# First attention of a three-stage kernel: from a generator-driven order to a sorted list of timed events, one slot per head

## Chip, cores, metric

The kernel runs on one core of a Trainium2 chip, as a single launch. The metric is the device time of that launch in microseconds; lower is better. Five queues of one core matter here: PE (TensorE, matmuls, with its weight loads shown apart as PEld), DVE (VectorE), ACT (ScalarE), POOL (GpSimd), and SP (SyncE), which here only issues DMAs. Each takes its own instructions in order, and they meet at semaphores.

## The reference, cut to what matters

Four batches of 576 positions. Stage one is causal attention with 8 heads of 64 and a cumulated log decay. Stage two adds a rank-32 mix over positions and a wide feed-forward layer. Stage three is a second attention of four gated experts. Only stage one and the first part of stage two are touched.

```python
def _attn_ref(q, k, v, f):              # q, k, v: (4, 8, 576, 64); f: (4, 8, 576)
    scores = scale * np.matmul(q, k.transpose(0, 1, 3, 2))
    cum = np.cumsum(np.log(np.clip(f, 0.0001, 1.0)), axis=-1)
    decay = cum[:, :, :, None] - cum[:, :, None, :]
    scores = np.where(causal, -1000000000.0, scores + decay)
    attn = np.exp(scores - np.max(scores, axis=-1, keepdims=True))
    attn = attn / (np.sum(attn, axis=-1, keepdims=True) + 1e-09)
    return np.matmul(attn, v)

def _moe_ref(x, U, V, w_ch1, w_ch2):    # x: (4, 576, 512), w_ch1: (512, 2048)
    h = x.transpose(0, 2, 1) @ U @ V
    u = x + h.transpose(0, 2, 1)
    return u + np.maximum(u @ w_ch1, 0.0) @ w_ch2
```

The results have to be good to far more than 16 bits, so operands are split in a high and a low part and multiplied in three products.

## The kernel before, in words

**Units of work.** There are 32 heads, taken as 16 pairs: the two heads of a pair share one load of q and k (`qkt`), one of v (`vr`) and one tile `x` for their result. The work of a head is:

- *split*: ACT writes the high parts of q and k, SP issues three or four DMAs that move halves to the other partitions and bring the decay sums, POOL subtracts to get the low parts (`split_high`, `split_low`);
- *row maxima* (`row_max`): PE computes unshifted scores of the rows in two PSUM tiles, `ua` (2 matmuls) and `ub` (4 matmuls), DVE takes their maxima (L174, L189), PE turns these (`mt`), DVE makes the row `mr` (L196) and SP writes it by DMA into the last partition of `qa` (L198), so that the score matmul subtracts the maximum;
- *scores*: PE fills two PSUM tiles `sc`, the first with 5 matmuls, the second with 12 (L232); ACT takes the exponentials (L242, three of them) and their 16-bit high parts `ph` (L247); DVE subtracts to get the low parts (L248);
- *attend*: 45 small matmuls (L263 to L267) into `av`, then three DVE operations `den`, `rn`, `x` (the last is L316) that normalise.

`ua`, `ub` and both `sc` share one pair of PSUM buffers (tag `s2`) in turn, so each of the four waits for the reader of the one two before it.

**Per pair** come the scaling of v (`am`, `amt`, `ar`, `rsp`, `rs`, `vr`, `vh`, `vl`: seven short steps that go from DVE to PE and back twice) and the *mix* of stage two (`mix`): `gp` (5 products in 10 passes) from `x`, then `g`, then `up` (7 matmuls), `ustage`, and a store of 288 KB to `udram`, which ACT's queue issues.

**Beside it** run two things. The weights of the first two quarters of the feed-forward layer come as 16 blocks of 512 KB of 8-byte numbers, which ACT (2 passes) and DVE (L353, L354) turn into 4-byte ones; the first eight are then split by ACT and POOL. And from pair 5 on, *fills* are put between the steps on PE: one fill is 12 matmuls of 288 columns of the feed-forward layer, either a hidden tile (`hps`, L638, read by ACT and DVE) or an output tile (`cps`, L654, read by DVE). `GROUPS` says how many fills a pair has, 38 in all. After stage one the same stream of fills goes on without attention, the dense phase, in which the next quarter's operands are made ready, paced by the fills.

**What sets the order.** `first_batch` (pairs 0 to 3) and `later_batches` (pairs 4 to 15) are written as generators that are advanced step by step; PE keeps that order, the others (DVE, ACT, POOL, SP) are put in order by a scheduler that ranks what is ready. In the later pairs one copy of `qkt`, `vr` and `x` is in use, in the first four pairs two. In the later pairs the mix of a pair is put between the two score tiles of the head after next, and the blocks of weights come in bunches per pair: `WRATE` gives 2, 3 and 3 to pairs 2, 3, 4, one to each of pairs 5 to 12, and the rest are eight small maxima.

Of the kernel before, what the change touches and what calls it, by code (L numbers as in the profile page):

```python
# [8 lines left out]
F32 = mybir.dt.float32  # L9
# [9 lines left out]
P = 128  # L19
# [45 lines left out]
def kernel(  # L65
# [100 lines left out]
    def row_max(hb, mx, apart=False):  # L166

# [3 lines left out]
        for c0, c1 in ((0, HC), (HC, S)):  # L171
            nc.tensor.matmul(ua[:, c0 // HC, 0:HC], qa[0:AUG, M_LO[4]:S], ka[0:AUG, c0:c1],
                             start=True, stop=True)
        nc.vector.tensor_tensor_reduce(  # L174
            ua[:, :, 0:HC], ua[:, :, 0:HC],
            maskm[:].rearrange("p (c n) -> p c n", c=2), 1.0, NEG, OP.add, OP.max, mx[:, 4:5])
        if apart:
            yield
        ub = ps2.tile([P, 2, 512], F32, name="ub", tag="s2")
        where = {3: (0, 0), 0: (0, 448), 2: (1, 0), 1: (1, 320)}  # L180
        for t in (3, 2, 1, 0):
            bk, off = where[t]
            w = M_W[t]
            nc.tensor.matmul(ub[:, bk, off:off + w], hb.wide[0:AUG, t * P:t * P + P],  # L184
                             ka[0:AUG, 0:w], start=True, stop=True)
        for t in (3, 2, 1, 0):
# [5 lines left out]
        yield  # L192
        mt = psf.tile([NT, P], F32, name="mt", tag="f")
        nc.tensor.transpose(mt[:], mx[:], ident[:])
        mr = small.tile([NT, P], F32R, name="mr", bufs=2)
        cur["mr"] = nc.vector.tensor_scalar(mr[:], mt[:], PSCALE_LN / ISC, None, OP.subtract)  # L196
        row = f32(hb.wide[AUG:P, :]).rearrange("o (t p) -> o t p", p=P)
        cur["last"] = nc.sync.dma_start(row, f32(mr[:]))  # L198

# [8 lines left out]

    def scores(hb, exps, select=False):

        qa, qb, ka, kb = hb
        ph, pl = exps
        for u in range(2):
            ps = ps2.tile([P, 2, 512], F32, name="sc", tag="s2")
            if u == 0:
                pieces = ((0, 0, 0, HC, 0), (0, HC, 1, HC, 0))
            else:
                pieces = ((2, 256, 0, 320, 0), (3, 384, 0, 192, 320),
                          (1, 128, 1, 448, 0), (4, 512, 1, 64, 448))

            todo = []
            for some in (pieces[:-1], pieces[-1:]):
                todo += [(ka[:, jt * P:jt * P + P], qa[:, i0:i0 + w], bk, off, w)
                         for jt, i0, bk, w, off in some]
                todo += [(kb[:, jt * P:jt * P + P], qb[:, i0:i0 + w], bk, off, w)
                         for jt, i0, bk, w, off in some]
            if not select:
                todo += [(identb[:], maskt[:, 0:min(P, w)], bk, off, min(P, w))
                         for jt, i0, bk, w, off in reversed(pieces) if i0 == jt * P]
            banks = [t[2] for t in todo]  # L230
            for n, (wa, xa, bk, off, w) in enumerate(todo):
                nc.tensor.matmul(ps[:, bk, off:off + w], wa, xa, start=bk not in banks[:n],  # L232
                                 stop=bk not in banks[n + 1:])
            if u == 0:
                todo = ((ps[:, :, 0:HC], 0, S, ((0, P),)),)
            else:
                todo = ((ps[:, 0, :], S, 512, ((0, P), (320, P))),
                        (ps[:, 1, :], S + 512, 512, ((0, P), (448, 64))))
            for view, o0, n, diagonals in todo:
                pf = cur["pf"].tile([P, S], F32, name="pf")  # L240
                pfv = pf[:, 0:S].rearrange("p (c n) -> p c n", c=2) if u == 0 else pf[:, 0:n]
                nc.scalar.activation(pfv, view, AF.Exp, scale=ISC)  # L242
                for d0, w in diagonals if select else ():
# [27 lines left out]
    def value_scale(vr):  # L271
# [3 lines left out]
        yield  # L275
        at_ = psf.tile([1, P], F32, name="amt", tag="f")
        nc.tensor.transpose(at_[:], am[:], ident[:])
        counter[1] += 1
# [6 lines left out]
        yield  # L285

        rp = psf.tile([P, 1], F32, name="rsp", tag="f")
        nc.tensor.matmul(rp[:], every[:], full[:].bitcast(BF16)[:, 1:2], start=True, stop=True)
        rs = small.tile([P, 1], F32, name="rs")
# [3 lines left out]
    def value_parts(vr, rs, vh, vl):  # L293

        scaled = nc.vector.tensor_scalar(vr, vr, rs[:, 0:1], VEXP, OP.mult, OP.mult)
        nc.scalar.copy(vh[:, :, :, 0:64], vr)
        nc.gpsimd.tensor_tensor(vl[:], vr, vh[:, :, :, 0:64], OP.subtract)
        return scaled
# [33 lines left out]
    def narrow(wt, raw, n, p0=0, p1=P):  # L332


        lo, hi = raw[p0:p1, :, 0], raw[p0:p1, :, 1]
        wi = wt.bitcast(I32)
        nc.vector.tensor_scalar(wi, lo, 29, None, OP.logical_shift_right)
        nc.scalar.activation(f32(lo), f32(hi), AF.Copy, scale=2.0 ** -112)
        nc.vector.scalar_tensor_tensor(wi, lo, 3, wi, OP.logical_shift_left, OP.bitwise_or)
        nc.vector.scalar_tensor_tensor(wi, hi, -2147483648, wi, OP.bitwise_and, OP.bitwise_or)  # L340

    def low_bits(wt, raw):

# [12 lines left out]
    def load_quarter_steps(wp, q):  # L356
# [1274 lines left out]
```

## Time and profile before

| | |
|---|---|
| device time, median of 3 runs (lowest, highest) | 904.18 us (900.08, 904.35) |
| the profiled execution: its own time, its span | 904.51 us, 902.8 us |
| stage one: first exponential of head 0, of head 31, last matmul of the last mix | 21.72, 362.28, 377.1 us |
| mean distance from head to head in stage one | 340.56 us / 31 = 10.99 us |
| PE busy, DVE busy over the span | 780.2 us, 634.3 us |

The span is the time from the first to the last instruction; the execution's own time is 1.7 us longer. Busy time counts an engine as busy while at least one of its instructions runs. Matmuls overlap each other, so the cost of one is read from the distance of two starts, not from its duration. PEclk is the granted clock of TensorE, 1.00 being the full 2.4 GHz and 0.50 the lower level.

### The profile page before, as it was taken

What the parts mean: (1) busy time and instruction counts of PE and PEld (TensorE: products, weight loads), DVE (VectorE), ACT (ScalarE), POOL (GpSimd) and SP (SyncE); (2) the same over time, 40 slices, a digit from 0 to 9 for tenths busy, and PEclk for the clock granted to TensorE, in tenths of its full rate; (3) what the DMA queues carried; (4) which work ended last, traced back from release to release, by engine and by line L of the source; (5) the groups of instructions that cost most, each with busy time, mean ns of one, the idle gap of its engine ahead of it and who ended that gap; (6) DMA issues with size and microseconds to landing.
All of it is one profiled execution on the core that took longest, in us unless ns stands there. A gap on an engine that the chain in (4) does not pass through costs nothing.

```text
span 902.8 us, 19100 instructions
## 1 busy us (share of the span) xinstructions
PE 780.2 (86%) x7426; PEld 666.0 (74%) x7426; DVE 634.3 (70%) x1716; ACT 440.0 (49%) x852; POOL 211.5 (23%) x297
## 2 busy tenths in 40 slices
PE   3687576767877887989989999999999999889997
PEld 2676576666877786889767777777777888777764
DVE  6999986676567656279778737746653688887875
ACT  4587764455555554246262313311321267576674
POOL 9856753243433430000000100000001131011110
PEclk9997998999899999999999999999999999989999
DMA  6346653445444421159263231440010251412212
GB/s 189 111 111 175 177 160 103 112 131 170 112 137 132 125 72 40 31 190 311 78 194 100 93 117 28 158 147 1 1 54 27 57 155 29 113 35 73 48 66 94
DMA packets 59210, 96.05 MB, mean 106 GB/s; under 512 B 4928, under 2 KB 39088, under 8 KB 59120
## 3 DMA queue, kind: packets, MB, share of 16 engines
q1 hardware_dynamic: 54560, 86.06, 32.3%
q10 hardware_dynamic: 4560, 8.78, 2.7%
q8 instruction: 58, 0.95, 0.5%
q14 instruction: 32, 0.26, 0.1%
HBM read 53.26 MB, written 23.74 MB: 85 GB/s over the span
## 4 chain that ended last, share of the span: by engine, by line
PE 43%; DVE 6%; DMA 1%; ACT 1%; issue 1%; POOL 0%; SPq 0%; DVEq 0%; POOLq 0%
PE cps L654 15%; PE hps L638 14%; PE pq L1273 3%; PE pv L1325 3%; PE po L1359 3%; PE sc L232 2%; PE ub L184 1%; DVE ub L189 1%; DVE ph L248 1%; DMA raw<-in_w_dram 1%; PE av L263 1%; PE av L267 1%; PE av L265 1%; DVE qb L1288 1%; DMA yst<-ydram 0%
## 5 line engine op out<-in xcount | busy, mean ns | idle before, releaser
L642 ACT ACTIVATE hh<-hps 128x288 f16<-128x288 f32 (+1 forms) x128 | 52.5, 410 | 211.9 <-PE hps L638 189.0
L248 DVE TENSOR_TENSOR ph<-pf,ph 128x576 f16<-128x576 f32 x144 | 121.7, 849 | 34.6 <-ACT ph L247 34.3
L643 DVE SCALAR_TENSOR_TENSOR hl<-hps,hh 128x288 f16<-128x288 f32 (+1 forms) x128 | 58.1, 454 | 83.1 <-ACT hh L642 82.6
L232 PE MATMUL sc<-qa,ka 128*128 128x288 f32 (+4 forms) x288 | 81.1, 343 | 37.1 <-DMA qa<-mr 11.5
L242 ACT ACTIVATE pf<-sc 128x576 f32<-128x576 f32 x144 | 84.5, 611 | 45.0 <-PE sc L232 40.3
L247 ACT CAST ph<-pf 128x576 f16<-128x576 f32 x144 | 89.2, 635 | 6.1 <-POOL pf L244 4.7
L189 DVE CUSTOM_DVE_ANT_0 ub<-ub,maskm 128x448 f32<-128x448 f32 x192 | 81.4, 424 | 15.1 <-PE ub L184 8.6
L232 PEld LDWEIGHTS sc<-qa,ka 128*128 128x128 f32 x288 | 55.0, 212 | 45.3 <-DVE mx L189 12.6
L263 PE MATMUL av<-vh,ph 128*128 128x65 f16 x720 | 73.4, 198 | 0.3 <-DVE x L316 0.3
L267 PE MATMUL av<-vh,ph 128*128 128x65 f16 x720 | 73.3, 196 | 0.0
L265 PE MATMUL av<-vl,ph 128*128 128x64 f16 x720 | 73.3, 195 | 0.0
L232 PE MATMUL sc<-qb,kb 128*128 128x288 f32 (+4 forms) x288 | 70.3, 327 | 0.0
L263 PEld LDWEIGHTS <-ph 128*128 128x128 f16 x720 | 67.4, 99 | 1.5 <-DVE x L316 0.5
L265 PEld LDWEIGHTS <-ph 128*128 128x128 f16 x720 | 67.5, 101 | 0.7
L267 PEld LDWEIGHTS <-ph 128*128 128x128 f16 x720 | 67.6, 99 | 0.0
L659 DVE SCALAR_TENSOR_TENSOR yc<-cps,back,yc 128x288 f32<-128x288 f32 x96 | 49.4, 514 | 25.3 <-PE cps L654 22.6
L232 PEld LDWEIGHTS sc<-qb,kb 128*128 128x128 f32 x288 | 58.9, 212 | 2.0
L184 PE MATMUL ub<-ka,qa 127*128 127x448 f32 x192 | 38.7, 327 | 22.4 <-ACT pf L242 11.2
L184 PEld LDWEIGHTS ub<-ka,qa 127*128 127x128 f32 x192 | 33.9, 207 | 28.2 <-ACT pf L242 13.1
L244 POOL TENSOR_SCALAR_AFFINE_SELECT pf<-pf 128x128 f32<-128x128 f32 (+1 forms) x80 | 21.8, 299 | 127.6 <-ACT pf L242 110.7
L654 PE MATMUL cps<-hh,w16b 128*128 128x288 f16 x256 | 48.3, 286 | 0.8 <-DVE hl L643 0.8
L654 PE MATMUL cps<-hh,w16a 128*128 128x288 f16 x256 | 48.4, 286 | 0.0
(245 smaller groups left out, 2286.1 us busy)
## 6 DMA issues: line engine op xcount, KB each, us to landing
raw<-in_w_dram SPq DMA_DIRECT2D x32, 512.0 KB
qkt<-in_qk_dram SPq DMA_DIRECT2D x16, 576.0 KB
ust<-udram SPq DMA_DIRECT2D x14, 576.0 KB
ydram<-yc SPq DMA_DIRECT2D x10, 576.0 KB
vr<-in_v_dram SPq DMA_DIRECT2D x16, 320.0 KB
udram<-ustage ACTq DMA_DIRECT2D x16, 288.0 KB
ydram<-ust SPq DMA_DIRECT2D x8, 576.0 KB
yc<-ydram SPq DMA_DIRECT2D x8, 576.0 KB
```

Source lines behind the costliest of these rows:

```text
L184: nc.tensor.matmul(ub[:, bk, off:off + w], hb.wide[0:AUG, t * P:t * P + P], ka[0:AUG, 0:w], start=True, stop=True)
L189: nc.vector.tensor_tensor_reduce(ub[:, bk, off:off + w], ub[:, bk, off:off + w], maskm[:, S - w:S], 1.0, NEG, OP.add, OP.max, mx[:, t:t + 1])
L232: nc.tensor.matmul(ps[:, bk, off:off + w], wa, xa, start=bk not in banks[:n], stop=bk not in banks[n + 1:])
L242: nc.scalar.activation(pfv, view, AF.Exp, scale=ISC)
L247: nc.scalar.copy(ph[:, o0:o0 + n], pf[:, 0:n])
L248: nc.vector.tensor_tensor(pl[:, o0:o0 + n], pf[:, 0:n], ph[:, o0:o0 + n], OP.subtract)
L263: nc.tensor.matmul(av[:, it, :], ph[:, c:c + P], vh[:, jt, :], start=first, stop=False)
L265: nc.tensor.matmul(av[:, it, 0:64], ph[:, c:c + P], vl[:, jt, :], start=False, stop=False)
L267: nc.tensor.matmul(av[:, it, :], pl[:, c:c + P], vh[:, jt, :], start=False, stop=last)
L638: nc.tensor.matmul(ph[:], wa[:, k, fs], xa[:, k], start=n == 0, stop=n == 3 * KT - 1)
L643: nc.vector.scalar_tensor_tensor(hl[:], ph[:], 0.0, hh[:] if dt == F16 else f32(hh[:]), OP.max, OP.subtract)
L654: nc.tensor.matmul(pc[:], wa[:, t, dsl], xa[:], start=n == 0, stop=n == 3 * FT - 1)
```

## The change

The order of stage one is no longer written by generators. Every step of the work becomes an event with a time, `h * SLOT + us`, with SLOT = 8.4; the events of all heads, pairs, blocks of weights and fills go in one list, which is sorted by time and then run. All five queues, POOL included, keep the order in which the sorted list issues. The times only sort: nothing in the program waits for a clock.

What else changes with it: q, k, v and `x` of two pairs have room throughout (`places`), three buffers of exponentials are used in turn, and two instead of three pairs of `ph` are there in the first pairs; the two parts of the row maxima stand together; the mix of pair p stands late in the two slots that follow its last head; one block of weights per head in slots 2 to 9, then one in every second slot; the readers of a fill (`hh`, `hl`, `yc`) get places of their own; the store to `udram` is issued by SP; 40 fills are in stage one, the last four of them behind the last head. ACT also makes the low bits of the mix's own weights, which DVE made before.

```diff
-WRATE = (0, 0, 2, 3, 3) + (1,) * 8 + (3, 3, 2)
-SPREAD = {0: (), 3: (2, 5, 8), 4: (2, 4, 6, 8)}
-GROUPS = (0,) * 5 + (3, 3, 3, 3, 4, 4, 4, 4, 3, 4, 3)
+SLOT = 8.4
+PER_PAIR = (0,) * 5 + (3, 3, 3, 3, 4, 4, 4, 4, 3, 3, 2)
...
+    def put(h, us, do, *what):
+        events.append((h * SLOT + us, len(events), do, what))
...
+        put(h, 0.0, products, 0)
+        put(h, 0.6, products, 1)
+        for n, (te, th, tl) in enumerate(((0.75, 1.35, 2.0), (2.2, 3.35, 4.25),
+                                          (2.75, 3.95, 5.0))):
+            put(h, te, exp_, n)
+            put(h, th, lambda n: high_part(ph, *st["pf", n]), n)
+            put(h, tl, lambda n: low_part(ph, pl, *st["pf", n]), n)
...
+        put(h + 1, 2.15, attend)
+        put(h + 1, 3.6, finish)
...
+            put(h - 2, 5.1, rows, 0)
+            put(h - 2, 5.4, rows, 1)
+            put(h - 2, 6.15, lambda: last_max(st[0], st["mx"]))
+            put(h - 2, 6.85, lambda: first_max(st[1], st["mx"]))
...
+        put(h - 1, 2.05, turn)
+        put(h - 1, 2.75, lambda: put_row(hb, st["mt"]))
...
+            put(h, 5.6, split_high, p, j)
+            put(h, 6.9, split_moves, p, j)
+            put(h, 6.9, split_low, p, j, (0,))
+            put(h, 9.4 if j else 8.3, split_low, p, j, (1,))
+        put(2 * (p - 2) - 1 if p > 2 else 0, 0.1, load_qk, p)
+        put(2 * (p - 2), 2.0, load_v, p)
...
+        put(h, 6.0, begin)
+        put(h, 6.85, lambda: mix_high(st["gp"]))
+        put(h, 8.4, lambda: mix_low(st["gp"]))
+        put(h + 1, 5.95, turn, 0)
+        put(h + 1, 6.5, turn, 1)
...
+        put(h + 1, 7.8, lambda: mix_store(p, st["ust"]))
+        put(h + 1, 10.8, parts, True)
...
+        put(h - 1, 7.9, read)
+        put(h, 7.1, lambda: low_bits(st["to"], pairs_of_words(st["raw"])))
+        put(h + 1, 0.7, lambda: join_bits(st["to"], pairs_of_words(st["raw"])))
...
+        for n, (j, us, ta, td) in enumerate(((0, 3.5, 5.2, 5.75), (1, 3.5, 5.2, 5.75),
+                                             (0, 6.6, 8.3, 8.75), (1, 7.2, 8.4, 8.75))):
+            if n < PER_PAIR[p]:
+                fill_events(2 * p + j, us, ta, td)
+    for t in range(2 * FT):
+        weight_events(0, t, t + 2)
+        weight_events(1, t, 2 * (t + 5))
...
+    with tc.manual_schedule(engines=IN_ORDER | {mybir.EngineType.Pool}):
+        for _, _, do, what in sorted(events, key=lambda event: event[:2]):
+            do(*what)
...
-    with tc.manual_schedule(engines={mybir.EngineType.PE}):
-        later_batches(*first_batch(m_first))
```

On PE, the place of the ninth mix. Before, it stands between the two score tiles of a head: the transpose of v's maximum (`amt`), then `gp`, then the second score tile.

```order
L232 LDWEIGHTS identb
L232 MATMUL sc<-maskt,identb 128x128
L277 MATMUL amt<-ident,am 1x128
L842 MATMUL gp<-x,ut 96x128 x5
L232 MATMUL sc<-qa_145,ka_147 128x320
L232 MATMUL sc<-qa_145,ka_147 128x192
L232 MATMUL sc<-qa_145,ka_147 128x448
L232 MATMUL sc<-qb_146,kb_148 128x320
L232 MATMUL sc<-qb_146,kb_148 128x192
```

Now the same mix (its input `x` is the part of the tile `aside` that holds a pair's result) follows the row maxima of a later head and stands ahead of a fill.

```order
L170 MATMUL ua<-ka_135,qa_133 128x288 x2
L188 MATMUL ub<-ka_135,qa_133 128x448
L188 MATMUL ub<-ka_135,qa_133 128x320
L188 MATMUL ub<-ka_135,qa_133 128x192
L188 MATMUL ub<-ka_135,qa_133 128x64
L335 LDWEIGHTS every
L335 MATMUL rsp<-ar_84,every 128x1
L835 MATMUL gp<-aside,ut 96x128 x5
L648 MATMUL cps<-hh,w2h 128x288
```

The mix has moved out from between the two score tiles; a fill, not the head's own scores, is what stands behind it.

On DVE, in the middle of a head of pair 9 to 10. Before, the three operations that normalise (`den`, `rn`, then `x`) are spread among the row maxima and a fill's sum.

```order
L248 TENSOR_TENSOR ph_173<-pf,ph_173 128x512
L305 TENSOR_SCALAR den<-av,rs 128x5
L189 ISA ub,mx_96<-ub,maskm 128x320
L189 ISA mx_96 128x1
L657 TENSOR_TENSOR ust<-cps,ust 128x288
L310 RECIPROCAL rn<-den 128x5
L189 ISA ub,mx_96<-ub,maskm 128x192
```

Now they stand together, ahead of the last two low parts of the exponentials, and the maxima come as one block behind those.

```order
L354 TENSOR_SCALAR den<-av,rs 128x5
L359 RECIPROCAL rn<-den 128x5
L365 TENSOR_TENSOR room<-av,rn 128x5x64
L277 TENSOR_TENSOR ph_170<-pf,ph_170 128x512
L277 TENSOR_TENSOR ph_170<-aside,ph_170 128x512
L638 SCALAR_TENSOR_TENSOR hl<-hps,hh 128x288
L175 ISA ua,mx_96<-ua,maskm 128x2x288
L175 ISA mx_96 128x1
L196 ISA ub,mx_96<-ub,maskm 128x448
```

The maxima have moved behind all that the head itself needs.

## Rows read from the trace of the kernel before

**Rows 1.** The page: span, and PE and DVE (busy us, share, instructions).

```profile
span 902.8 us, 19100 instructions
PE 780.2 (86%) x7426; PEld 666.0 (74%) x7426; DVE 634.3 (70%) x1716; ACT 440.0 (49%) x852; POOL 211.5 (23%) x297
```

**Rows 2.** ACT by time: the first exponential of head 0 and head 31.

```profile
21.72 0.65 ACT L242 ACTIVATE pf<-sc 128x576 f32<-128x576 f32 x1
...
362.28 0.65 ACT L242 ACTIVATE pf<-sc 128x576 f32<-128x576 f32 x1 [4.49 <-PE sc L232]
```

**Rows 3.** Stretches: length, busy PE, PEld, DVE, ACT, POOL, PEclk, DMA share, GB/s.

```profile
48.47:68.51 20.04, 17.50 (x238) 15.91 (x238) 19.68 (x69) 16.67 (x33) 10.52 (x8) 1.00 0.41 116
...
75.90:86.20 10.30, 8.54 (x72) 7.95 (x73) 9.79 (x21) 9.41 (x20) 8.25 (x7) 0.50 0.45 123
...
136.09:362.28 226.19, 173.55 (x1874) 162.47 (x1875) 147.66 (x435) 119.35 (x221) 75.90 (x49) 0.93 0.39 112
...
377.00:415.80 38.80, 36.41 (x276) 35.94 (x275) 27.49 (x68) 16.22 (x31) 0.00 (x0) 1.00 0.63 203
```

**Rows 4.** Waits, 22 to 378 us: waiter, releaser, us in total, times, longest.

```profile
PE gp L842 <- DVE x L316: 14.3, 8, 3.8
PE ub L184 <- ACT pf L242: 11.2, 7, 2.6
...
PE sc L232 <- DMA qa<-mr: 8.9, 6, 2.9
...
PE sc L232 <- DVE mx L189: 8.4, 7, 2.7
```

**Rows 5.** PE by time, heads 17 to 19: start, us, instruction, idle before it.

```profile
212.85 0.73 PE L232 MATMUL sc<-qa,ka 128*128 128x320 f32 x3 [0.58 <-DVE mx L189]
...
214.22 0.38 PE L638 MATMUL hps<-uh,w1h 128*128 128x288 f32 x1
...
215.89 0.27 PE L194 MATMUL mt<-ident,mx 128*5 128x128 f32 x1
...
217.80 0.75 PE L184 MATMUL ub<-ka,qa 127*128 127x448 f32 x4 [1.36 <-ACT pf L242]
218.39 0.21 PE L263 MATMUL av<-vh,ph 128*128 128x65 f16 x1
...
219.77 0.38 PE L654 MATMUL cps<-hh,w2h 128*128 128x288 f32 x1
...
227.03 2.45 PE L842 MATMUL gp<-x,ut 128*96 128x128 f32 x10 [3.80 <-DVE x L316]
```

**Rows 6.** PE by time: a `gp` and an `up` at full clock.

```profile
275.52 1.33 PE L842 MATMUL gp<-x,ut 128*96 128x128 f32 x10 [1.89 <-DVE x L316]
276.61 0.71 PE L232 MATMUL sc<-qa,ka 128*128 128x320 f32 x3
...
303.17 0.38 PE L850 MATMUL up<-ident,x 128*128 128x128 f32 x2
...
304.23 0.43 PE L172 MATMUL ua<-ka,qa 127*128 127x288 f32 x2
```

**Rows 7.** DVE groups, 22 to 378 us: busy us, mean ns of one | idle before.

```profile
L643 DVE SCALAR_TENSOR_TENSOR hl<-hps,hh 128x288 fp32r<-128x288 f32 x21 | 9.4, 448 | 2.3 <-ACT hh L642 2.1
...
L354 DVE SCALAR_TENSOR_TENSOR w32a<-raw,w32a 128x512 int32<-128x512 int32 x8 | 5.7, 718 | 0.1
```

**Rows 8.** The low parts on DVE: ns of one, least, median, most.

```profile
L248 DVE TENSOR_TENSOR ph<-pf,ph x144: 645/693/4129, 24.3 to 888.8; 128x512 f16<-128x512 f32 x96, 128x576 f16<-128x576 f32 x48
```

**Rows 9.** POOL and DVE by time around that longest one.

```profile
79.78 1.75 POOL L811 TENSOR_TENSOR kb<-qkt,ka 64x576 fp32r<-64x576 f32 x1
...
83.01 3.00 POOL L391 TENSOR_TENSOR w1l<-wst,w1h 128x512 fp32r<-128x512 f32 x2
...
80.76 4.13 DVE L248 TENSOR_TENSOR ph<-pf,ph 128x576 f16<-128x576 f32 x1 [0.50 <-ACT ph L247]
```

**Rows 10.** SP's own longest wait, 22 to 378 us.

```profile
SPq L611 <- DMA udram<-ustage: 12.4, 2, 11.0
```

More of the change, by code (lines that the diff above doesn't have):

```diff
@@ new lines, in score_views, with exponentials @@
+    def score_views(ps, u):
+        if u == 0:
+            return ((ps[:, :, 0:HC], 0, S, ((0, P),)),)
+        return ((ps[:, 0, :], S, 512, ((0, P), (320, P))),
+                (ps[:, 1, :], S + 512, 512, ((0, P), (448, 64))))
+    def exponentials(view, n):
+        if "turn" in cur:
+            cur["turn"].append(cur["turn"].pop(0))
+            pf = cur["turn"][0]
+        else:
+            pf = cur["pf"].tile([P, S], F32, name="pf")
+        whole = n == S
+        nc.scalar.activation(pf[:, 0:S].rearrange("p (c n) -> p c n", c=2) if whole
+                             else pf[:, 0:n], view, AF.Exp, scale=ISC)
+        return pf
@@ L209, in scores, with high_part, low_part @@
+    def high_part(ph, pf, o0, n):
+        nc.scalar.copy(ph[:, o0:o0 + n], pf[:, 0:n])
+    def low_part(ph, pl, pf, o0, n):
+        nc.vector.tensor_tensor(pl[:, o0:o0 + n], pf[:, 0:n], ph[:, o0:o0 + n], OP.subtract)
     def scores(hb, exps, select=False):
-        qa, qb, ka, kb = hb
         ph, pl = exps
         for u in range(2):
[L214 to L242, printed above, removed]
@@ L243, in scores @@
+            ps = score_products(hb, u, select)
+            for view, o0, n, diagonals in score_views(ps, u):
+                pf = exponentials(view, n)
                 for d0, w in diagonals if select else ():
@@ L826, in one, with mix_sums @@
+        for n in which:
+            dst, src, high = todo[n]
+            nc.gpsimd.tensor_tensor(dst, src, f32(high), OP.subtract)
     def one(gen):
         next(gen, None)
-    def attend(p, j):
-        vh, vl = vhs[p % 2]
-        ph, pl = st_p[p, j]
-        av = weighted_values(ph, pl, vh[:, j], vl[:, j])
-        rn = row_scales(av, st_rs[p])
-        normalise(xs[p][:, :, j * D:j * D + D], av, rn)
-    def mix(p):
-        b, m, x = p // NP, p % NP, xs[p]
+    def mix_sums(p):
         gp = psf.tile([3 * R, P], F32, name="gp", tag="f")
+        x = places[p % 2][2]
@@ new lines, in mix_turn, with mix_copy @@
+    def mix_turn(p, i):
+        t0, t1, c0, c1 = TURNS[i]
+        x = places[p % 2][2]
+        up = psf.tile([P, 512], F32, name="up", tag="f")
+        for t in range(t0, t1):
+            nc.tensor.matmul(up[:, t * P - c0:t * P - c0 + P], x[:, t, :], ident[:],
+                             is_transpose=True, start=t == t0, stop=False)
+        nc.tensor.matmul(up[:, 0:c1 - c0], g[:], vs[:, c0:c1], start=False, stop=True)
+        return up
+    def mix_copy(ust, up, i):
+        t0, t1, c0, c1 = TURNS[i]
+        nc.scalar.copy(ust[:, c0:c1], up[:, 0:c1 - c0])
@@ new lines, in largest_event, with largest_of, fill_events, products @@
+    def largest_event(t, h):
+        def largest_of():
+            if t == 0:
+                largest[1] = small.tile([P, 2, FT], F32, name="wam0", bufs=1)
+            nc.vector.tensor_reduce(largest[1][:, t // FT, t % FT:t % FT + 1], w32[1][:, t, :],
+                                    AX.X, OP.max, apply_absolute_value=True)
+        put(h, 0.7, largest_of)
+    def fill_events(h, us, t_act, t_dve):
+        mine = []
+        def products():
+            fill(1)
+            mine.extend(deferred)
+            del deferred[:]
+        def run(n):
+            for some in mine:
+                some[n]()
+        put(h, us, products)
+        put(h, t_act, run, 0)
+        put(h, t_dve, run, 1)
```

660 lines of the change are left out of this document (343 added, 317 removed).

## Prediction

> **What bounds the kernel now.** I began with the page [rows 1]: no engine is full, PE is busy 780.2 of 902.8 us and DVE 634.3. So the question is whether stage one, the only stage whose order changes, is held by an engine or by waits. Head 0's first exponential starts at 21.72 us, head 31's at 362.28 us [rows 2]: 340.56 us for 31 heads, 10.99 us each. The stretches tell two different stories [rows 3]. From 48.47 to 68.51 us, three heads without fills and without blocks of weights, DVE is busy 19.68 of 20.04 us: 6.68 us a head, DVE-bound. From 136.09 to 362.28 us, nineteen heads with fills, 11.9 us each, DVE is busy 147.66 of 226.19 us and PE 173.55: both idle, PE for 52.6 us or 2.77 us a head. There the end is set by hand-offs. The view of waits names them [rows 4]: `gp` waits for the normalised `x` (14.3 us), `ub` for the exponentials that free its buffer (11.2), score tiles for the row's DMA (8.9) and for the maxima (8.4). The timeline shows one: `gp` stands idle 3.80 us for DVE while fills that need nothing are behind it in PE's queue [rows 5]. And the granted clock is 0.93 over that stretch and 0.50 from 75.90 to 86.20 us, so the gaps also make the work behind them slower [rows 3].
>
> **What the change costs and removes.** Almost no arithmetic goes; the order is what changes. So I work out how long a slot must be on the fuller engine, and add what hand-offs leave.
>
> *PE per slot, at full clock.* A fill: from 214.22 to the next start at 215.89, 1.67 us; the second score tile 212.85 to 214.22, 1.37; `ub` 217.80 to 218.39, 0.59; attend 218.39 to 219.77, 1.38 [rows 5]. `gp` takes 275.52 to 276.61, 1.09, and `up` 303.17 to 304.23, 1.06 [rows 6]. The first score tile (5 matmuls) and `ua` (2) I estimate from the fill's 1.67/12 = 0.14 each: 0.7 and 0.3. A slot's own work is then 0.7 + 1.37 + 1.38 + 0.3 + 0.59 + 1.08 (the mean of `gp` and `up`) = 5.4 us, 7.1 with one fill, 8.75 with two.
>
> *DVE per slot.* 6.56 us busy a head without fills and blocks (19.68/3) [rows 3]. A block of weights adds two operations of 0.72 (L354; L353 is alike), 1.4 us [rows 7]; a fill one operation over 288 columns, which I put at 0.45 from that 0.72 for 512.
>
> *Slots without fills (0 to 9).* DVE sets them: 6.7 us, plus 1.4 for a block or, in the first three, for the mix's own weights: 8.1. POOL runs under DVE here, and I add 0.3 for that (below): 8.4 x 10 = 84 us. ACT, 16.67 us in those three heads or 5.6 each [rows 3], has 2.5 us left for the block's three passes of about 0.7, which it hides; the slots would become longer by what exceeds that.
>
> *Slots 10 to 17* have two fills and one in turn: 8.75 on PE, then 7.1 on PE against 6.56 + 0.45 + 1.4 = 8.4 on DVE: 8.6 x 8 = 69 us. *Slots 18 to 25* have two fills each: 8.75 on PE against 6.56 + 0.9 + 0.7 = 8.2 on DVE: 70 us. *Slots 26 to 30*: two fills in two of them, one in three, eight small maxima of 0.7 at most: 2 x 8.75 + 3 x 7.7 = 41 us. Sum over the 31 distances: 264 us, 8.5 each.
>
> *Hand-offs.* The trace has two ends: 0.12 us a head where DVE is full ((20.04 - 19.68)/3) and 2.77 on PE where nothing is [rows 3]. In the new order what stands between two uses of a tile on one engine is other work: attend and a fill (3.0 us) between the second score tile and `ub`, so that three exponentials and their high parts pass under them; the maxima behind all low parts, so that `mr` leaves early in a slot and its row has some 5 us to land before the next score tile. The three longest waits of rows 4 so lose their cause. I take 0.5 a head, near the full end: 16 us, in sum 280 us instead of 340.6, a gain of 60.6.
>
> *Ends.* Before head 0 nothing of weight changes: 0, give or take 2. Behind head 31's exponential, before: 14.7 us to the last mix. After: 5.5 us rest of its slot, then attend, `gp`, `up` and four fills, 1.38 + 1.09 + 1.06 + 4 x 1.67 = 10.2: 1.0 us more. But stage one now does 40 fills for 38. The dense phase behind it is PE-bound, busy 36.41 of 38.80 us up to 415.8 [rows 3], so two fills less save 3.3 us there; if its DVE work, paced by the same fills, became late, they would save nothing.
>
> *What the moved DMAs do.* SP now also issues the 16 stores to `udram`, and waits in program order. Behind a waiting store or load stand the row of the next head, the split moves and the next block. The longest such wait is 11.0 us [rows 10]; once a batch it would hold up a row whose slack is 5 us, 6 us late, three times in all: 0 to 18 us. I take 0, near the bulk of rows (PE waited 8.9 us in all for rows, in six waits [rows 4]), and keep 18 for the range.
>
> Sum, against the profiled execution of 904.5 us, which is 0.3 above the median of the runs: 904.5 - 60.6 + 1.0 - 3.3 = 841.6. I say 841 us. With hand-offs of 0.12 it is 830, with 1.2 863: the likeliest case's own range.
>
> **A rule that speaks against it.** The low part of an exponential takes 693 ns at the median and 4,129 ns once [rows 8], and that one started at 80.76 us between POOL operations that followed each other without a break until past 84 us [rows 9]. DVE was held for 3.4 us. The new order puts the same POOL work in 8.4 us instead of 11; it gives POOL places from 5.2 us of a slot on, where DVE reads PSUM, but in slots 3 to 9 POOL has splits, weights, v and mix, at 1.4 to 1.8 us an operation some 7 us in every second slot, which run into the low parts of the next.
>
> The Trainium skill, "SBUF — State Buffer", section "Who interferes with whom", says that a DVE instruction with two SBUF inputs and a GpSimd instruction that reads SBUF exclude each other, and that the later one blocks fully until the other is through. By that rule the trace agrees, and the hold is a lock that comes back in every slot where POOL is late, the second rival below; by the median of 693 ns it is rare, and 0.3 us a slot is enough.
>
> **Rivals.**
>
> *The waits stay.* Five queues in one fixed order wait for the slowest hand-off of each slot, and the scheduler that could put other work in front is gone; then PE keeps its 2.77 us of idle time. For it: nineteen heads in which PE's order was already fixed. Against: the causes of the three longest waits are moved apart. 2.77 instead of 0.5 is 2.27 x 31 = 70 us: 912, no gain at all; half of it, which I find likelier, is 877.
>
> *POOL holds DVE.* In slots 3 to 9 one low part per slot is held for 3.4 us [rows 8, 9], and 0.3 of that is in the sum already: 7 x 3.1 = 22 us: 863. For it: POOL 10.52 us busy even in the three light heads [rows 3]. Against: the block of maxima, which reads PSUM, now stands where POOL's places are.
>
> *Slower: the row comes last.* With every queue in order, `mr` goes out only when SP has issued what is ahead of it; if SP is held each slot, the row's landing becomes the slot's length. From a start at 3 us of the slot, a landing 8.6 us later makes a slot of 11.6, and 31 x (11.6 - 9.0) = 80 us more than the forecast: 921. It decides from 11.0 us a slot, when the row lands 8 us after `mr`. For it: the wait of 11.0 us on SP [rows 10]. Against: PE's longest wait for a row was 2.9 us [rows 4].
>
> *It gains more.* If the full clock holds throughout and hand-offs vanish: 264 us for 31 heads, 826 less what the contention estimate was too high, 820.
>
> **How the numbers follow.** Forecast (826 to 863) 0.62; waits stay, by half or wholly, 0.15, a third of which ends within 0.5% or above; POOL holds DVE 0.10; gains more 0.06; slower by the row 0.07. The predicted time is 841. For 8 times in 10 the range runs from 820, where the gains end, to 877, the half case of the first rival; about 0.12 lies above and 0.06 below. Within 0.5% is what a measurement of this kernel can't tell from no change. Faster: 0.62 + 0.10 + 0.10 + 0.06 = 0.88; same 0.04; slower 0.08.
>
> **What would show it.** Right: the distance of the first exponentials falls to about 9 us and is even; PE's waits for `x`, the exponentials and the maxima shrink to under 15 us together; from slot 10 on PE is busy over 90% with the clock near 1.00; the mix of a pair never leaves PE idle for 3 us; the dense phase is as long as before less two fills. Wrong: DVE's low parts with a mean near 1 us and more in slots 3 to 9 (POOL); score tiles that wait for the row with SP held (the slower rival); PE idle for 2 us and more in each slot behind one and the same releaser (the waits stay). The forecast is wrong if the last mix ends later than 345 us.

## The result and the profile after

The changed kernel takes 879.78 us (median of 4 runs, 875.88 to 882.09) against 903.22 us before (4 runs): a ratio of 0.974, interval 0.970 to 0.979. Faster, but 39 us slower than forecast, and beyond the upper end of the range. Only stage one moved: from head 0's first exponential to head 31's it is 318.89 us now and 340.56 before, and from there to the end of the span 540.1 and 540.5.

The page, as [rows 1], and ACT's first exponentials of heads 0, 10 and 31, as [rows 2]:

```profile
span 880.4 us, 19124 instructions
PE 783.0 (89%) x7426; PEld 672.8 (76%) x7426; DVE 667.4 (76%) x1713; ACT 443.4 (50%) x857; POOL 214.2 (24%) x298
```

```profile
21.43 0.65 ACT L269 ACTIVATE aside<-sc 128x576 f32<-128x576 f32 x1 [6.76 <-PE sc L250]
...
134.62 0.65 ACT L269 ACTIVATE aside<-sc 128x576 f32<-128x576 f32 x1 [0.76 <-PE sc L250]
...
340.32 0.65 ACT L269 ACTIVATE aside<-sc 128x576 f32<-128x576 f32 x1 [0.34 <-DVE g L842]
```

DVE does the same work and is busy 33 us longer than in [rows 1]; some 12 of these are there too in the two runs below in which POOL reads nothing (626.1 us with the change, 613.7 in the kernel before), so not all of it is what follows. Slots 0 to 9 are 11.3 us each where 8.9 were forecast (113.19 for 89 us), slots 10 to 30 are 9.8 where 9.1 were (205.70 for 191).

The stretches of the changed kernel, with the columns of [rows 3]: slots 0 to 9, slots 10 to 30, and six slots in the middle of these.

```profile
21.43:134.62 113.19, 76.93 (x723) 69.28 (x722) 98.62 (x215) 72.72 (x136) 68.06 (x52) 0.82 0.43 129
134.62:340.32 205.70, 183.70 (x2064) 175.98 (x2065) 185.07 (x484) 132.23 (x247) 83.36 (x57) 0.93 0.46 133
227.30:282.18 54.88, 52.50 (x617) 50.56 (x617) 52.06 (x142) 40.53 (x76) 25.67 (x17) 1.00 0.58 168
```

The six slots in the middle, 19 to 24, are what was forecast: 9.15 us each, PE busy 96% at full clock. In slots 0 to 9 DVE is busy 98.62 of 113.19 us, so it is the engine that sets them, and PE, idle for a third, runs at a granted clock of 0.82.

What became longer on DVE are above all the low parts of the exponentials, the operation of [rows 8]. All 93 of them in stage one, DVE's busy time in them (fourth number), first of the kernel before, then of the changed one:

```profile
21.72:362.28 340.56, 85.97 (x93) 0.92 0.43 124
```

```profile
21.43:340.32 318.89, 97.64 (x93) 0.89 0.45 131
```

Free of POOL, one of 512 columns takes 0.68 us and one of 576 takes 0.75, so that 62 and 31 of them need 65.4 us. The rest is time in which DVE stands inside the instruction, called the hold from here on: 20.6 us before, 32.2 after. The six middle slots have their share of it; their 18 low parts take 16.86 us where 12.7 would do:

```profile
227.30:282.18 54.88, 16.86 (x18) 1.00 0.58 168
```

PE sets these slots, so the 4.2 us don't show in their length. By form, slots 0 to 9 of the changed kernel (DVE groups, columns as in [rows 7]): the last low part of each head takes 1.79 us at the mean.

```profile
L277 DVE TENSOR_TENSOR ph<-aside,ph 128x512 f16<-128x512 f32 x10 | 17.9, 1792 | 0.0
L277 DVE TENSOR_TENSOR ph<-pf,ph 128x512 f16<-128x512 f32 x10 | 12.6, 1256 | 0.6 <-ACT ph L274 0.6
L277 DVE TENSOR_TENSOR ph<-aside,ph 128x576 f16<-128x576 f32 x10 | 8.7, 873 | 3.6 <-ACT ph L274 3.6
L175 DVE CUSTOM_DVE_ANT_0 ua<-ua,maskm 128x576 f32<-128x576 f32 x10 | 7.5, 752 | 0.0
```

One such slot by time, all engines (L824 is a split on POOL, L277 a low part, L175 the first of the maxima that frees the score tile's place, L250 the next score tile):

```profile
94.05 0.22 DVE L354 TENSOR_SCALAR den<-av,rs 128x5 f32<-128x5 f32 x1 [0.98 <-PE av L309]
...
94.82 1.40 POOL L824 TENSOR_TENSOR qb<-room,qa 64x576 fp32r<-64x576 f32 x1
94.94 1.83 DVE L277 TENSOR_TENSOR ph<-pf,ph 128x512 f16<-128x512 f32 x1
96.30 1.74 POOL L824 TENSOR_TENSOR kb<-room,ka 64x576 fp32r<-64x576 f32 x1
96.70 1.89 DVE L277 TENSOR_TENSOR ph<-aside,ph 128x512 f16<-128x512 f32 x1
98.51 0.75 DVE L175 CUSTOM_DVE_ANT_0 ua<-ua,maskm 128x576 f32<-128x576 f32 x1
...
99.38 0.40 PE L250 MATMUL sc<-qa,ka 128*128 128x288 f32 x1 [2.97 <-DVE mx L175]
```

Read it from the POOL rows: the split runs from 94.82 to 96.22, the low part that began beside it ends 0.55 us later; the next split runs from 96.30 to 98.04, the next low part ends 0.55 us behind that. Each low part waits for one POOL operation and then does its work. The maxima stand behind them, and PE waits 2.97 us for the first of these. DVE also stood 0.98 us at `den`, for attend, with both low parts queued behind it.

The waits, as [rows 4], from 21.4 to 362 us:

```profile
PE sc L250 <- DVE mx L175: 38.0, 16, 3.8
...
DVE den L354 <- PE av L309: 21.6, 22, 2.1
...
PE sc L250 <- ACT aside L269: 7.4, 10, 0.7
...
PE gp L835 <- DVE aside L365: 0.3, 1, 0.3
```

`gp`'s wait for `x`, 14.3 us before, is gone; so is `ub`'s for the exponentials (11.2 us) and that for the row (8.9). What is left for exponentials is the score tiles' 7.4 us. One wait has taken their place, that for the maxima: 38.0 us.

### The profile page after: what moved, and what is told of

It reads as the page before. It is cut to its first block, busy times and chain, and to the rows that moved or that the text cites. A ratio compares the mean times of both kernels' runs of the same rounds, so it can differ in the third digit from the quotient of the medians.

```text
span 880.4 us, 19124 instructions
## 1 busy us (share of the span) xinstructions
PE 783.0 (89%) x7426; PEld 672.8 (76%) x7426; DVE 667.4 (76%) x1713; ACT 443.4 (50%) x857; POOL 214.2 (24%) x298
## 4 chain that ended last, share of the span: by engine, by line
PE 44%; DVE 6%; DMA 1%; ACT 1%; issue 1%; POOL 0%; SPq 0%; DVEq 0%; POOLq 0%
PE cps L648 15%; PE hps L632 14%; PE pq L1425 4%; PE pv L1477 3%; PE po L1511 3%; PE sc L250 2%; PE ub L188 1%; DVE ub L196 1%; DVE ph L277 1%; DMA raw<-in_w_dram 1%; PE av L305 1%; PE av L309 1%; PE av L307 1%; DVE qb L1440 1%; DMA yst<-ydram 0%
## 5 line engine op out<-in xcount | busy, mean ns | idle before, releaser
L250 PE MATMUL sc<-qa,ka 128*128 128x288 f32 (+4 forms) x288 | 83.3, 351 | 54.1 <-DVE mx L175 38.0
L250 PEld LDWEIGHTS sc<-qa,ka 128*128 128x128 f32 x288 | 56.3, 218 | 63.0 <-DVE mx L175 41.5
L305 PE MATMUL av<-vh,ph 128*128 128x65 f16 x720 | 82.3, 206 | 0.0
L309 PE MATMUL av<-vh,ph 128*128 128x65 f16 x720 | 81.5, 204 | 0.7 <-DVE ph L277 0.7
L307 PE MATMUL av<-vl,ph 128*128 128x64 f16 x720 | 81.8, 204 | 0.0
L277 DVE TENSOR_TENSOR ph<-aside,ph 128x576 f16<-128x576 f32 x64 | 74.5, 1164 | 5.3 <-ACT ph L274 5.2
L307 PEld LDWEIGHTS <-ph 128*128 128x128 f16 x720 | 72.9, 107 | 1.7
L305 PEld LDWEIGHTS <-ph 128*128 128x128 f16 x720 | 73.0, 105 | 1.4 <-issue 0.4
L309 PEld LDWEIGHTS <-ph 128*128 128x128 f16 x720 | 72.5, 105 | 0.9 <-DVE ph L277 0.9
L250 PE MATMUL sc<-qb,kb 128*128 128x288 f32 (+4 forms) x288 | 72.8, 337 | 0.0
L277 DVE TENSOR_TENSOR ph<-pf,ph 128x512 f16<-128x512 f32 (+1 forms) x80 | 62.6, 786 | 9.6 <-ACT ph L274 9.4
L269 ACT ACTIVATE pf<-sc 128x512 f32<-128x512 f32 (+1 forms) x80 | 47.3, 606 | 39.0 <-PE sc L250 37.9
L269 ACT ACTIVATE aside<-sc 128x576 f32<-128x576 f32 x64 | 39.7, 621 | 48.3 <-PE sc L250 47.9
L250 PEld LDWEIGHTS sc<-qb,kb 128*128 128x128 f32 x288 | 61.1, 220 | 2.3
L287 POOL TENSOR_SCALAR_AFFINE_SELECT pf<-pf 128x128 f32<-128x128 f32 (+1 forms) x80 | 21.6, 296 | 127.5 <-ACT pf L269 110.5
L274 ACT CAST ph<-pf 128x512 f16<-128x512 f32 (+1 forms) x80 | 49.4, 630 | 5.0 <-POOL pf L287 4.2
```

The lines of the kernel that those rows point to most:

```text
L269: nc.scalar.activation(pf[:, 0:S].rearrange("p (c n) -> p c n", c=2) if whole else pf[:, 0:n], view, AF.Exp, scale=ISC)
L305: nc.tensor.matmul(av[:, it, :], ph[:, c:c + P], vh[:, jt, :], start=first, stop=False)
L307: nc.tensor.matmul(av[:, it, 0:64], ph[:, c:c + P], vl[:, jt, :], start=False, stop=False)
L309: nc.tensor.matmul(av[:, it, :], pl[:, c:c + P], vh[:, jt, :], start=False, stop=last)
```

## The experiments

Three theories. A: the clock is the root; without fills PE idles and falls to half clock, attend comes late, DVE with it, and the low parts fall onto POOL. B: POOL is the root; each of its operations that reads SBUF holds a low part, whatever the clock is. C: DVE's own order is the root; it stands at `den` for attend with other work behind. With each run goes one number, DVE's busy time in the 93 low parts of stage one: 97.6 us in the changed kernel, 65.4 when free.

**The clock alone.**

```diff
+    def idle_products():
+        pw = psf.tile([P, HC], F32, name="pw", tag="f")
+        for n in range(12):
+            nc.tensor.matmul(pw[:], identb[:], maskm[:, 0:HC], start=n == 0, stop=n == 11)
+    for h in range(10):
+        put(h, 3.5, idle_products)
+        put(h, 6.6, idle_products)
```

> Twelve products over 288 columns that nothing uses are put where slots 0 to 9 have no fill (at 3.5 and 6.6 us of the slot), so that PE is not idle there and its clock stays up; nothing else changes. Theory A (the root is PE's clock: without fills PE idles 3.8 us in each of slots 0 to 9, runs at half clock, attend and the second score tile come late, so the normalisation and the low parts behind it come late and fall onto POOL): the second score tile takes 1.4 us instead of 2.5, attend ends earlier, slots 0 to 9 fall from 11.3 to about 9.5 us, 18 us less in all: about 862 us, and the mean of the 20 low parts there falls from 1.52 us to below 1.1. Theory B (the root is POOL, which blocks DVE whatever the clock is): the clock rises to 1.0, PE is no longer idle, but DVE's low parts stay near 1.5 us and slots 0 to 9 stay at 10.8 to 11.3: 875 to 880 us. Theory C (DVE's own order: normalisation ahead of the low parts, and dependent operations one behind the other): between, some 4 us off by an earlier attend, 876 us.

872.0 us (869.7 to 873.0), ratio to before 0.964: between A's 862 and B's 875. Slots 0 to 9:

```profile
21.58:127.23 105.65, 86.69 (x963) 75.58 (x962) 98.92 (x219) 72.70 (x136) 65.10 (x51) 0.97 0.46 136
```

The clock went from 0.82 to 0.97 and the slots from 11.3 to 10.6 us, but DVE is as busy as before (98.92 us) and the low parts take 98.5 us in all: A falls as the root. The clock has a share, 8 us, and the trace shows where: DVE's wait at `den` in stage one is 8.5 us, 20.0 in the changed kernel.

**POOL reads nothing.**

```diff
-        put(h + 1, 5.2, lambda: nc.gpsimd.tensor_tensor(vl[:], vr, vh[:, :, :, 0:64], OP.subtract))
+        put(h + 1, 5.2, lambda: nc.gpsimd.memset(vl[:], 0.0))
...
-            nc.gpsimd.tensor_tensor(dst, src, f32(high), OP.subtract)
+            if p < 2:
+                nc.gpsimd.tensor_tensor(dst, src, f32(high), OP.subtract)
+            else:
+                nc.gpsimd.memset(f32(dst), 0.0)
```

and the same for the low parts of the weights, the mix and the hidden batches.

> POOL's subtractions of stage one (low parts of q and k from pair 2 on, of v, of the feed-forward weights, of the mix and of the hidden batches) become a fill with zeros of the same tile: POOL still writes the tile in its place, but reads nothing; the low parts are left out of the result. Theory B (POOL's reading of SBUF blocks DVE): DVE's low parts fall to 0.69 to 0.75 us each, which takes away the 24 us of excess in slots 0 to 9 and 20 in slots 10 to 31, as far as DVE is what sets the slot: slots 0 to 9 near 9.3 us, and no slot of 12 us at 16, 17 and 25: 840 to 850 us. Theory A (clock): slots 0 to 9 keep PE idle and half clock, about 10.3 us, 10 us less there, and some 8 us in the three cascades: 862 us. Theory C: slots 0 to 9 stay at 11, only the cascades go: 870 us.

836.1 us (835.7 to 838.9), ratio 0.925, below B's own 840. Stage one as a whole, and the low parts in it:

```profile
21.23:297.81 276.58, 240.56 (x2787) 227.37 (x2787) 242.12 (x698) 204.36 (x383) 65.38 (x108) 0.96 0.53 152
```

```profile
21.23:297.81 276.58, 65.33 (x93) 0.96 0.53 152
```

DVE is busy 242.1 us where it was 283.7 (98.62 + 185.07), 41.6 less, and the time is 43.7 less. Of the 41.6, 32.3 lie in the low parts, some 7 in the 32 block operations (22.1 us here, 29.0 in the changed kernel), the rest in the same operations on the mix's weights. The low parts are free, though POOL still writes the same tiles. The six middle slots are hardly shorter without the hold, 54.38 us where they were 54.88:

```profile
193.97:248.35 54.38, 52.86 (x617) 51.73 (x617) 47.76 (x141) 40.57 (x76) 11.98 (x18) 0.98 0.56 160
```

A fill is also shorter and waits for no copy on ACT, so this run alone could be read as POOL being earlier. Against that: in the changed kernel's stage one neither PE nor DVE has a wait that POOL ends. And the next two keep POOL's work whole; the second makes POOL wait for DVE.

**Normalisation behind the low parts.**

```diff
-        put(h + 1, 3.6, finish)
+        put(h + 1, 5.6, finish)
```

> The normalisation of a head (den, rn, x) is put behind the low parts of the next head (5.6 us of the slot instead of 3.6). Theory C (DVE stands at den for attend while two low parts that need nothing of it are queued behind it): DVE's wait for av falls from 21.6 us to under 5, and with it the time by 12 to 17 us: 863 to 868 us; the mix's gp, which needs x, comes 2 us later in every second slot and costs a few us from slot 8 on. Theory A and B: the low parts start about 1 us earlier and miss part of POOL's work, 5 to 10 us less in slots 0 to 9: 870 to 875 us.

844.35 us (842.7 to 846.0), ratio 0.934, interval 0.930 to 0.937: 35 us from one number, twice what C said and far more than A and B. By time, a slot like the one above, DVE and then POOL:

```profile
90.00 0.67 DVE L277 TENSOR_TENSOR ph<-pf,ph 128x512 f16<-128x512 f32 x1
90.59 0.67 DVE L277 TENSOR_TENSOR ph<-aside,ph 128x512 f16<-128x512 f32 x1
91.20 0.20 DVE L354 TENSOR_SCALAR den<-av,rs 128x5 f32<-128x5 f32 x1
...
92.07 0.76 DVE L175 CUSTOM_DVE_ANT_0 ua<-ua,maskm 128x576 f32<-128x576 f32 x1
...
94.70 1.05 DVE L392 SCALAR_TENSOR_TENSOR wst<-raw,wst 128x512 int32<-128x512 int32 x1
```

```profile
91.13 1.36 POOL L1027 TENSOR_TENSOR vl<-aside,vh 128x640 f16<-128x640 f32 x1 [4.14 <-issue]
92.45 1.26 POOL L1140 TENSOR_TENSOR w2l<-wst,w2h 128x512 fp32r<-128x512 f32 x1
93.80 1.41 POOL L824 TENSOR_TENSOR qb<-room,qb 64x576 fp32r<-64x576 f32 x1
```

The low parts are through at 91.26, just as POOL begins; its three operations now lie under the normalisation and the maxima, which read PSUM and take what they take alone (`ua` 0.76 here, 0.75 in the row above). Only the block's operation at 94.70 still meets a split. The low parts take 74.4 us, and `den` never waits in stage one.

**POOL waits for the last low part.**

```diff
+        def hold():
+            nc.gpsimd.tensor_copy(held[:], pl[0:1, S + 1022:S + 1024])
+
+        put(h, 5.15, hold)
```

> POOL copies two numbers of the last low part of each head in slots 0 to 31 before it goes on with the operations that stand at 5.2 us and later: so these cannot start before DVE's low parts of the slot are through. Theory B (POOL against DVE): the low parts at 2.75 and 5.0 us are free in every slot (0.69 and 0.75 us), only the first one can still meet POOL's rest: excess in slots 0 to 9 falls from 24 to about 8 us, time 860 us. Theory A: the same low parts are free, but PE's idle time and half clock stay: 868 us. If POOL's work has too little room behind the gate (7 us in every second slot), it comes late for v and for the splits, and PE waits for it: 885 us.

851.5 us (849.3 to 854.5), ratio 0.941, below all three forecasts; low parts 70.4 us, clock in stage one 0.91. DVE still stands at `den` (12.8 us), and the clock is as low as it was, but the time falls by 28 us: B, by a second way that leaves all work in.

**Both together: is it one thing?** The edits of the second and third run.

```diff
-        put(h + 1, 3.6, finish)
+        put(h + 1, 5.6, finish)
...
-            nc.gpsimd.tensor_tensor(dst, src, f32(high), OP.subtract)
+                nc.gpsimd.memset(f32(dst), 0.0)
```

> Both edits together: normalisation behind the low parts, and POOL's subtractions of stage one replaced by a fill with zeros (low parts left out, as before). Each alone took 35 and 44 us off. If both work through the same thing, POOL blocking DVE's low parts (theory B), there is nothing left for the second edit to take: 832 to 838 us. If the late normalisation works through DVE's order itself (theory C: DVE no longer stands at den), the gains add: about 800 to 815 us.

833.4 us (832.5 to 837.1). The late normalisation is worth 35 us with POOL reading and 2.7 without, where the two ratios to before have intervals that overlap (0.920 to 0.929 and 0.922 to 0.928). So C alone is worth 3 us at most, and 32 of the 35 need POOL's reads. They are not all hold: from the changed to the late kernel DVE's busy time in stage one falls by 24.5 us (283.7 to 259.2), its idle time by 13.3 (35.2 to 21.9), and the wait at `den`, 20.0 us, is what went from the latter. With POOL holding DVE, that wait counts as well.

**The kernel before without POOL's reads.** The same replacement in the old kernel.

```diff
-        nc.gpsimd.tensor_tensor(vl[:], vr, vh[:, :, :, 0:64], OP.subtract)
+        nc.gpsimd.memset(vl[:], 0.0)
```

> The kernel before with the same replacement of POOL's subtractions in stage one by a fill with zeros (low parts left out). There DVE is idle a third of the time from head 12 on, and the excess of its low parts over their free durations is 20 us in stage one against 35 with the change. Theory B: the block costs the kernel before less, because it falls on idle time of DVE: 888 to 898 us; the change without the block is then worth 52 to 62 us (to 836), about what was forecast for it, and the rest of the forecast went into the block. If the kernel before gains as much as the changed one (near 860 us), the block explains nothing of the miss.

880.3 us (877.2 to 884.2), ratio 0.976; low parts 66.6 us. That is 22 us less, where B said 5 to 15, but the 22 can't be put down to the hold. The kernel before leaves DVE's, ACT's and POOL's order to the scheduler, and with the fills it chose another one. In the kernel before, `den` stands behind both low parts of a head:

```profile
39.64 1.83 DVE L248 TENSOR_TENSOR ph<-pf,ph 128x512 f16<-128x512 f32 x1
...
41.55 0.21 DVE L305 TENSOR_SCALAR den<-av,rs 128x5 f32<-128x5 f32 x1
```

In this run the same `den` stands between them:

```profile
41.57 0.21 DVE L305 TENSOR_SCALAR den<-av,rs 128x5 f32<-128x5 f32 x1
41.71 0.67 DVE L248 TENSOR_TENSOR ph<-pf,ph 128x512 f16<-128x512 f32 x1
```

Nor do the gains lie where the hold was: slots 0 to 9 had 11 us of it in the low parts and became 2.1 us shorter (90.28 to 88.14), slots 10 to 30 had 10 and became 25.7 shorter (250.28 to 224.55). What the hold cost the kernel before stays open. What stands is the pair of times: where POOL reads nothing the change is worth 880.3 - 836.1 = 44 us, where it reads 23.

**Parts of the hold.** Only the splits, then only v, of the second run's replacement.

```diff
-            nc.gpsimd.tensor_tensor(dst, src, f32(high), OP.subtract)
+                nc.gpsimd.memset(f32(dst), 0.0)
```

```diff
-        put(h + 1, 5.2, lambda: nc.gpsimd.tensor_tensor(vl[:], vr, vh[:, :, :, 0:64], OP.subtract))
+        put(h + 1, 5.2, lambda: nc.gpsimd.memset(vl[:], 0.0))
```

> Only the splits' subtractions (q and k of pairs 2 to 15) become a fill with zeros, their low parts left out; v, weights, mix and hidden batches keep theirs. In the changed kernel's trace 18.6 of the 42.4 us by which DVE's low parts and block operations exceed their free durations begin under a split and 15.2 under v. Theory B with each hold paid for by itself: 1.1 us of time per us of hold, as with all of them: 880 - 20 = 860 us. Theory B with a phase (one hold makes the next): with fewer POOL operations the late phase is not kept up and nearly all goes: 842 to 850 us.

> Only the subtraction of v, in every second slot, becomes a fill with zeros (low part of v left out). Each hold by itself: 15.2 us of hold: 863 us. With a phase: 845 to 855 us, and the holds under splits fall as well though nothing is changed there; if the holds only move to the next POOL operation, which now starts where v's did: 875 us.

864.4 us (861.9 to 864.9) and 865.3 us (859.0 to 870.1); low parts 86.1 and 81.7 us. Each hold is paid by itself: 15.4 and 14.5 us, near the 20 and 17 expected, and no collapse by a phase. The other 14 of the 44 are left, by subtraction, to the weights', the mix's and the hidden batches' operations and to what the two share; no run takes these alone.

**More on top of the late normalisation**: POOL's wait, the unused products, and POOL's operations in pieces.

```diff
-            nc.gpsimd.tensor_tensor(dst, src, f32(high), OP.subtract)
+            for c in (slice(0, HC), slice(HC, S)):
+                nc.gpsimd.tensor_tensor(dst[:, c], src[:, c], f32(high[:, c]), OP.subtract)
```

> The late normalisation and POOL's wait for the last low part of a head together, nothing left out. Theory B: with the normalisation behind the low parts, the last of these ends about 1 us earlier, so POOL's wait costs less, and the low parts that still meet POOL in the late-normalisation kernel (6 of 24 of 512 columns held in slots 0 to 9) come free; the first low part and the block's two operations still meet POOL's rest: 838 to 844 us. Against it: POOL, held until the last low part, runs into the next slot's first low part more often: 846 to 850 us.

> The late normalisation together with the unused products that keep PE's clock up in slots 0 to 9. With the normalisation out of DVE's way, slots 0 to 9 are DVE's (idle 0.3 to 0.5 us of 9): theory B: the clock is worth nothing more: 842 to 846 us. Theory A: the half clock in slots 2, 5, 6 and 8 is what keeps them at 10 us: 836 to 840 us.

> The late normalisation, and POOL's long operations cut: a split and v in two halves, the hidden batch's low part in three; same work, nothing left out. A DVE operation that meets POOL then waits at most for a piece of about 0.75 us. Theory B (the later one waits for the other's end): the excess of 18.5 us falls to about 9, the time to 836 to 840 us. If DVE has to wait for all pieces that stand in POOL's queue (4.1 us once in the kernel before): excess 18 or more, 844 to 848 us.

847.7, 846.7 and 846.9 us: none is faster than 844.35. POOL's wait came out as its second case. The clock's 8 us are gone: with the normalisation late, DVE has no wait at `den` left for it to shorten. Pieces were expected to halve the hold and did not: the low parts take 76.7 us. By time, DVE and POOL in that kernel:

```profile
108.31 1.35 DVE L277 TENSOR_TENSOR ph<-aside,ph 128x576 f16<-128x576 f32 x1
...
109.91 0.95 DVE L277 TENSOR_TENSOR ph<-pf,ph 128x512 f16<-128x512 f32 x1
110.78 1.25 DVE L277 TENSOR_TENSOR ph<-aside,ph 128x512 f16<-128x512 f32 x1
```

```profile
106.91 2.14 POOL L825 TENSOR_TENSOR kb<-aside,ka 64x288 fp32r<-64x288 f32 x2
109.40 2.07 POOL L1029 TENSOR_TENSOR vl<-room,vh 128x320 f16<-128x320 f32 x2 [0.35 <-ACT vh L1027]
```

Each POOL row is two pieces of about 1 us. A held low part gets in after one piece (0.95 and 1.25 us, not 1.8), but the next one meets the next piece. So the time is that of the case in which DVE waits for all pieces, but the trace shows it waiting for one at a time.

**POOL's order left to the scheduler**, one part of the change undone.

```diff
-    with tc.manual_schedule(engines=IN_ORDER | {mybir.EngineType.Pool}):
+    with tc.manual_schedule(engines=IN_ORDER):
```

> One part of the change undone: POOL's queue is left to the scheduler, the other four keep the program's order. It puts the mix's low parts between the two splits of a slot; v, the splits' first halves and the weights keep their places. Theory B: the holds are made by v and the splits, which do not move: 874 to 884 us. If POOL's fixed order is what makes its operations late: 860 us.

881.7 us (876.5 to 887.3), as B expected: the scheduler left v and the splits where the program has them, and the hold stayed (96.8 us). An order on POOL that moves those was not run.

All runs by the time that the low parts take in stage one:

| kernel | low parts, us | time, us |
|---|---|---|
| changed, no reads on POOL, normalisation early / late | 65.3 / 65.1 | 836.1 / 833.4 |
| changed, POOL waits | 70.4 | 851.5 |
| late normalisation, with unused products / alone / with POOL's wait / in pieces | 73.6 / 74.4 / 74.7 / 76.7 | 846.7 / 844.4 / 847.7 / 846.9 |
| changed, v / splits without reads | 81.7 / 86.1 | 865.3 / 864.4 |
| POOL left to the scheduler / changed / unused products | 96.8 / 97.6 / 98.5 | 881.7 / 879.8 / 872.0 |

## Why the prediction failed

*The step that failed* is "I add 0.3 for that": POOL's hold was put at 0.3 us in each of slots 0 to 9, 3 us in all, and at nothing from slot 10 on. It measured 44 us (879.8 to 836.1). Take it away and the rest of the sum holds in total: 31 distances of 277 us by the sum without the 3, 276.58 in the run in which POOL reads nothing; 838 us by the sum, 836.1 measured. That it is so near is in part luck: slots 0 to 9 take 92.4 us there for 86 by the sum, slots 10 to 30 184.2 for 191, and the two errors cancel. The likeliest mechanism was right, its largest unknown mis-sized.

*How it was mis-sized.* I read the median, 693 ns, and the longest, 4,129 [rows 8], and called the hold rare. The sum was in the same trace: 85.97 us in 93 low parts, 20 us more than 65.4. And I took DVE's length of a slot, 6.56 us, from three heads in which only two low parts are clearly held, by 1.4 us in all:

```profile
57.19 1.85 DVE L248 TENSOR_TENSOR ph<-pf,ph 128x576 f16<-128x576 f32 x1
...
64.30 1.05 DVE L248 TENSOR_TENSOR ph<-pf,ph 128x576 f16<-128x576 f32 x1
```

Then I let DVE set slots 0 to 9, where each us of hold makes a slot a us longer. With the 20.6 in place of the 3 the sum would have been 859, still 21 short.

*Why 32 us and not 20.* The change puts `den`, `rn` and `x` ahead of two low parts. These begin 0.9 us later by that work alone (`den` at 94.05, the low part at 94.94), and by DVE's wait for attend on top (21.6 us in 22 slots). By then POOL has the inputs of v and of the splits. I had seen the order and written of POOL's places "where DVE reads PSUM", but had put the low parts ahead of them by the table's times, not by what stands in front on DVE.

*The rule.* By the Trainium skill, "SBUF — State Buffer", section "Who interferes with whom", the hold is a lock between a DVE operation with two SBUF inputs and a POOL operation that reads SBUF, and not one that only writes. The runs agree on both halves: 97.64 us with reads, 65.33 with writes alone. I gave the rival that rests on it 0.10 and 863 us; it should have been the forecast, and longer: it also held slots 10 to 30.

*Point by point.* The distance "about 9 us and even": 9.15 in the six slots that PE sets, 11.3 in slots 0 to 9; late singles at 10, 16 to 18, 25 and 28. Those at 16, 17 and 25 come down where POOL reads nothing (12.7, 11.3 and 12.5 us to 10.5, 6.5 and 8.2), and the hold is seen in slot 17, where the hidden batch's 2.04-us operation on POOL holds the block's:

```profile
204.60 2.04 POOL L591 TENSOR_TENSOR ul<-ust,uh 128x864 fp32r<-128x864 f32 x1 [4.21 <-ACT uh L587]
204.74 2.45 DVE L392 SCALAR_TENSOR_TENSOR w32a<-raw,w32a 128x512 int32<-128x512 int32 x1
...
210.03 1.15 DVE L277 TENSOR_TENSOR ph<-pf,ph 128x512 f16<-128x512 f32 x1
211.11 1.88 DVE L277 TENSOR_TENSOR ph<-aside,ph 128x512 f16<-128x512 f32 x1
```

Slot 18 is late without the reads too (12.7 us, 2.0 of them PE's wait for a row), so its cause is another and stays open. Hand-offs for `x`, exponentials and rows: 0.5, 7.7 and 0 us, right. The maxima: wrong, 43.9 us, because they stand behind the held low parts; together 52 us where under 15 was the sign. PE over 90% from slot 10 at full clock: 89% and 0.93; 94% and 0.99 where POOL reads nothing. The sign set for POOL, low parts with a mean near 1 us, came: 1.3 us in slots 0 to 9. The mix never idling PE: right. Ends: forecast -2.3 us, measured -0.4 (540.1 for 540.5). SP's stores at 0: right, PE never waited for a row in this view; the slower rival did not occur. The rival "the waits stay" named 877 us, near the time. Its sign, PE idle for 2 us and more behind one releaser, shows in slots 0 to 9 (the first maxima, 27.8 us in ten waits), but not for its reason: the three longest waits of [rows 4] went, and in stage one that wait falls from 38.0 us to 15.0 when POOL reads nothing. The last mix ends at 354.5 us, past the 345 that I had set as the mark of a wrong forecast.

The best kernel here is the changed one with one number altered, the normalisation at 5.6: 844.35 us, 35 below the change. What is left in it of the hold, 9 us on the low parts and some on the blocks' operations, bounds the rest: 833 us without POOL's reads.

## What to carry to other kernels

Price a stall inside instructions by its sum over a group, busy time less count times the free duration, never by the median. Where the held engine sets the pace it is paid in full: in slots 0 to 9, 20.1 us less of DVE's busy time made them 20.8 us shorter. Where another engine does, it is hidden: in the six middle slots 4.2 us of it cost 0.5. Where two engines exclude each other, place the operations of one under those of the other that don't take part, and count what stands ahead of them in the queue, not the times in a table. When several runs take the same time off, put two together: what does not add up has a cause in common.

## What the runs showed of the hardware

The hold works both ways: v's subtraction takes 1.36 us beside the maxima (the row at 91.13 above) and 1.79 when it starts behind a low part that is already running and takes its free 0.68:

```profile
82.80 0.68 DVE L277 TENSOR_TENSOR ph<-pf,ph 128x512 f16<-128x512 f32 x1
82.91 1.79 POOL L1027 TENSOR_TENSOR vl<-room,vh 128x640 f16<-128x640 f32 x1 [8.58 <-issue]
```

An operation whose inputs are one whole SBUF tile and a column of factors (`rs`) can be held as well: v's scaling on DVE takes 0.55 us, but in the kernel with POOL's pieces 1.08, beside the pieces of `kb` that started at 106.91:

```profile
107.31 1.08 DVE L1025 TENSOR_SCALAR room<-room,rs 128x640 f32<-128x640 f32 x1
```

What a full clock for PE is worth hangs on DVE's order: 8 us with the early normalisation, through the wait at `den`, and nothing with the late one, though the granted clock in stage one rose there too (0.96 to 0.99).
